# Dealing attention pieces into an expert-layer kernel by need, loading the first weights ahead of other transfers, and a last chunk of 128 tokens laid on partitions

## The chip, the cores and the metric

The kernel runs on one core of one Trainium2 chip. A core has a matrix engine (PE, with its weight loads shown as PEld), a vector engine (DVE), a scalar engine (ACT), a general engine (POOL) and a queue engine (SP) that issues transfers. [...] The metric is device time in microseconds (us), lower is better. A gain or loss counts as one from 0.5% on.

## The reference, cut to what matters

Two blocks run one after the other. The first is a polynomial attention without softmax; its output, with the heads side by side, is the token matrix `x` of 4352 tokens by 128 columns. The second is a sum over four experts, each a two-layer network of inner width 1024, weighted by normalised probabilities of each token.

```python
# q, k, v: (4, 4, 1088, 32); S1, S2: (8, 32)
def phi(x):
    a = np.einsum('rd,bhsd->bhsr', S1, x)
    b = np.einsum('rd,bhsd->bhsr', S2, x)
    return np.einsum('bhsi,bhsj->bhsij', a, b).reshape(*x.shape[:-1], 64)
q_p, k_p = phi(q), phi(k)
kv = np.einsum('bhsf,bhsd->bhfd', k_p, v)
z = np.sum(k_p, axis=2)
num = np.einsum('bhsf,bhfd->bhsd', q_p, kv)
den = np.einsum('bhsf,bhf->bhs', q_p, z)[..., None] + 1e-06
x = (num / den).transpose(0, 2, 1, 3).reshape(4352, 128)
# domain_probs: (4352, 4); w1: (4, 128, 1024); w2: (4, 1024, 128)
p = domain_probs / (domain_probs.sum(-1, keepdims=True) + 1e-09)
out = sum(p[:, e:e+1] * (np.maximum(x @ w1[e], 0) @ w2[e]) for e in range(4))
```

## The kernel before, in words

All data are 32-bit floats. The order of work on each engine is the order in which the Python code emits it (`manual_schedule`); each engine goes through its own list and waits where an operand is not there yet, and everything behind the waiting instruction waits with it. DMA issues stand in the lists of SP and ACT in the same way.

**Expert layer.** The 4352 tokens are columns of `xT` (feature on the partition), cut into chunks: 256, 416, 416, six of 512, and 192. A chunk takes 16 steps, four for each expert; a step handles 256 of the 1024 hidden features. `first(i)` makes the hidden values: for two blocks `j` of 128 features, the product `h` (weights from `w1_sb`), its rectified copy on ACT (L587), and sums and differences of its two token halves on DVE (L571). `second(i)` multiplies them by `w2`: the two token halves and two feature blocks are combined so that seven half-width products stand in for eight. For that `w2s` holds sums of blocks of `w2`, made on POOL by `weight_sums` (L477). The loop emits `second` two steps behind `first` (`LA = 2`). After the four steps of an expert, `gather` copies the two accumulators `o0`, `o1` out on ACT (`ev`), combines them on POOL (`yz`, `ev`, `ct`), multiplies by the gate (the normalised probability, broadcast over partitions by a DMA) and adds to `total`. After the last expert `turn_back` transposes on DVE into `ob` (L651) and SP stores four strips for each batch touched (L655).

The last chunk is "plain": eight full products instead of seven halves, hidden values on DVE alone with the gate multiplied in (L578), all four experts summed in one accumulator, then one transpose and four DMAs, two on SP and two on ACT.

**Attention.** It fills `xT` ahead of the experts. `start()` does the keys of batch 0 and the first 256 tokens, before any expert step. The rest is a Python generator, `front()`, of 260 pieces: 17 for the keys of each later batch and 19 for each unit of 352 to 416 query columns. A piece is one or two instructions (or none, where a gap is left): the transposed queries `qT`, a product with `sq` (tile `f`), three shuffles and an addition on DVE (`qf`, `qb`, `qa`), four products `qp`, the matmuls `den` and `num`, then `dT`, `rc`, `rb` and at last the piece that writes the unit's columns of `xT` (L429). `work()` is called twice a step, after each block `j`, and takes one piece each time (in chunk 0 three pieces in two steps). Before a chunk begins, the loop makes sure of its columns:

```python
while have[0] < START[m] + CHUNKS[m]:
    next(pieces)
```

Those pieces then stand one behind the other in the lists, with no expert work between them. In the profile each f32 matmul has two rows of its own, so a step has 8 rows of `h` and 14 of `o` (8 in the plain chunk); in the order listings below each matmul stands once.

**Transfers at the start.** SP issues the loads of keys, queries and values, then `w1` of expert 0. It then stores the gates (two of four batches; ACT stores the other two), loads the gate of chunk 0, and only then `w2` of expert 0 and the other weights. POOL makes the four `w2s` sums of expert 0 first and then copies the small matrix `sq` (L522), which the second query unit needs.

## Time and profile before

| | |
|---|---|
| time, median of 3 runs | 515.83 us (515.75 to 517.74) |
| the profiled execution: its time, its span | 517.37 us, 515.5 us |
| PE busy | 497.6 us, 97% of the span |
| DVE, ACT, POOL busy | 328.8, 237.2, 232.4 us |
| mean granted PE clock | 0.987 of full speed |

The profile is of one execution. Its span runs from the first to the last instruction; 1.87 us lie around it. Busy shares say little where an engine waits only now and then: what counts is which engine the others wait for at a given place. PE is the engine with almost no idle time, so the reading is a search for the places at which it stands still or runs at a lower clock.

### The profile page before, as it was taken

How to read it: one execution, taken by the hardware profiler on the slowest of the kernel's cores; microseconds unless marked ns; L12 is line 12 of the kernel's file. 1: busy time of each engine (PE TensorE's matmuls, PEld its weight loads, DVE VectorE, ACT ScalarE, POOL GpSimd, SP SyncE). 2: the span in 40 equal slices, each digit the busy share in tenths (PEclk: the TensorE clock that was granted, in tenths of full speed). 3: DMA queues.
4: the chain of work that ended last, by engine and by line, in shares of the span. 5: the costliest groups of instructions: out<-in, count | busy, mean ns of one | idle time of the engine just before them, and what ended most of it. 6: DMA issues, size and time to landing. Idle time of an engine off the chain costs nothing.

```text
span 515.5 us, 10496 instructions
## 1 busy us (share of the span) xinstructions
PE 497.6 (97%) x4178; PEld 356.1 (69%) x4178; DVE 328.8 (64%) x772; ACT 237.2 (46%) x463; POOL 232.4 (45%) x262
## 2 busy tenths in 40 slices
PE   8799999999989999999969999999999999999997
PEld 5477887877745577777625567777777777777786
DVE  7597777586948647476655765557576665454443
ACT  3255456454535454545504455444454455555410
POOL 6565335443534354324442445543555264526560
PEclk9999999999989999999969999999999999999999
DMA  6960123021002202021000210021000300011000
GB/s 186 320 203 2 67 56 88 3 81 18 2 1 81 61 3 86 2 83 21 1 0 1 83 22 0 1 80 25 2 0 6 98 0 2 2 34 18 1 17 14
DMA packets 30176, 22.85 MB, mean 44 GB/s; under 512 B 20784, under 2 KB 27184, under 8 KB 29616
## 3 DMA queue, kind: packets, MB, share of 16 engines
q1 hardware_dynamic: 28912, 21.76, 14.7%
q8 instruction: 33, 0.54, 0.4%
q10 hardware_dynamic: 1216, 0.42, 0.3%
q14 instruction: 15, 0.12, 0.1%
HBM read 19.87 MB, written 2.31 MB: 43 GB/s over the span
## 4 chain that ended last, share of the span: by engine, by line
PE 67%; DVE 2%; POOL 2%; ACT 0%; issue 0%; POOLq 0%; DVEq 0%
PE h L172 35%; PE o L172 27%; PE f L172 3%; POOL ct L686 1%; PE den L172 1%; PE num L172 1%; DVE qp L395 1%; POOL ev L686 1%; DVE hid L571 0%; POOLq L761 0%; POOL total L686 0%; POOL yz L674 0%; ACT hid L587 0%; DVE rb L425 0%; DVE xT L429 0%
## 5 line engine op out<-in xcount | busy, mean ns | idle before, releaser
L571 DVE SCALAR_TENSOR_TENSOR hid<-h,hid 128x256 f32<-128x256 f32 (+4 forms) x432 | 205.4, 476 | 161.0 <-ACT hid L587 153.9
L172 PE MATMUL h<-xT,w_sb 128*64 128x512 f32 (+3 forms) x1280 | 300.3, 535 | 7.3 <-DVE xT L429 5.3
L587 ACT ACTIVATE hid<-h 128x512 f32<-128x512 f32 (+2 forms) x288 | 160.1, 556 | 227.3 <-PE h L172 174.9
L172 PE MATMUL o<-hid,w2s 128*64 128x256 f32 (+2 forms) x1152 | 227.1, 359 | 0.0
L172 PE MATMUL o<-hid,w_sb 128*64 128x256 f32 (+3 forms) x992 | 200.1, 355 | 0.0
L172 PEld LDWEIGHTS h<-xT,w_sb 128*64 128x64 f32 x1280 | 140.4, 138 | 67.7 <-issue 18.0
L172 PEld LDWEIGHTS o<-hid,w2s 128*64 128x64 f32 x1152 | 132.2, 137 | 33.2 <-issue 2.1
L172 PEld LDWEIGHTS o<-hid,w_sb 128*64 128x64 f32 x992 | 111.1, 137 | 29.6 <-issue 9.7
L686 POOL TENSOR_TENSOR ev<-yz,sh 64x256 f32<-64x256 f32 (+2 forms) x72 | 49.5, 687 | 170.4 <-ACT sh L689 167.6
L674 POOL TENSOR_TENSOR yz<-ev 128x512 f32<-128x512 f32 (+2 forms) x36 | 43.2, 1201 | 78.1 <-ACT ev L677 77.7
L686 POOL TENSOR_TENSOR ct<-ev 128x512 f32<-128x512 f32 (+2 forms) x36 | 42.3, 1176 | 2.8
L686 POOL TENSOR_TENSOR ct<-ct,gate 128x512 f32<-128x512 f32 (+2 forms) x27 | 33.1, 1226 | 2.1
L686 POOL TENSOR_TENSOR total<-total,ct 128x512 f32<-128x512 f32 (+2 forms) x27 | 32.7, 1211 | 2.1
L395 DVE TENSOR_TENSOR qp<-qa,qb 64x352 f32<-64x352 f32 (+2 forms) x44 | 31.9, 725 | 1.0
L676 ACT COPY ev<-o 128x512 f32<-128x512 f32 (+2 forms) x36 | 19.6, 545 | 15.3 <-PE o L172 15.1
L677 ACT COPY ev<-o 128x512 f32<-128x512 f32 (+2 forms) x36 | 19.7, 546 | 2.4 <-PE o L172 0.3
L172 PE MATMUL den<-qp,kvz 128*64 128x352 f32 (+3 forms) x48 | 13.9, 501 | 3.9 <-DVE qp L395 3.2
L578 DVE SCALAR_TENSOR_TENSOR hid<-h,gate 128x192 f32<-128x192 f32 x32 | 10.8, 355 | 10.0 <-PE h L172 9.7
L689 ACT COPY sh<-yz 64x256 f32<-64x256 f32 (+2 forms) x36 | 13.8, 382 | 2.3 <-POOL yz L674 1.5
L690 ACT COPY sh<-yz 64x256 f32<-64x256 f32 (+2 forms) x36 | 13.8, 383 | 0.9
L337 DVE TENSOR_TENSOR kp<-fs 128x256 f32<-128x256 f32 (+1 forms) x24 | 14.2, 590 | 0.0
L172 PE MATMUL num<-qp,kvz 128*64 128x352 f32 (+3 forms) x48 | 13.6, 497 | 0.0
(97 smaller groups left out, 218.7 us busy)
## 6 DMA issues: line engine op xcount, KB each, us to landing
w_sb<-in_moe_w_dram SPq DMA_DIRECT2D x8, 512.0 KB, 8.0
gate<-gates SPq DMA_DIRECT2D x4, 1024.0 KB, 4.7
kn<-in_k_dram SPq DMA_DIRECT2D x4, 544.0 KB, 3.9
qn<-in_q_dram SPq DMA_DIRECT2D x4, 544.0 KB, 3.7
vn<-in_v_dram SPq DMA_DIRECT2D x14, 128.0 KB, 4.4
gate<-gates SPq DMA_DIRECT2D x2, 832.0 KB
out_dram<-ob SPq DMA_DIRECT2D x16, 64.0 KB, 1.9
gate<-gates SPq DMA_DIRECT2D x1, 896.0 KB
```

What stands on the lines that cost most here:

```text
L172: nc.tensor.matmul(out(s), weights(s), moving(s), **flags)
L337: eng.tensor_tensor(out=_ap(kps[b], 0, P, 256 * t0 + P * p + 64 * x, [[256, n], [32, 2], [R, 4], [1, R]]), in0=in0, in1=_ap(fss[b], 0, P, ...
L395: nc.vector.tensor_tensor(out=qp[p][64 * x : 64 * x + 64, 0:n], in0=qa[64 * p : 64 * p + 64, 0:n], in1=qb[64 * p : 64 * p + 64, 0:n], op=A ...
L571: nc.vector.scalar_tensor_tensor(out=out, in0=src, scalar=0.0, in1=in1, op0=ALU.max, op1=ALU.subtract)
L578: nc.vector.scalar_tensor_tensor(out=by_blocks(hd, n, n * j), in0=by_blocks(hp, n), scalar=0.0, in1=gate_of(m, e), op0=ALU.max, op1=ALU.mult,)
L587: nc.scalar.activation(hd[:, n * j : n * j + n], hp[:, 0:n], ACTF.Relu)
L674: add = lambda out, in0, in1, op=ALU.add: nc.gpsimd.tensor_tensor(out=out, in0=in0, in1=in1, op=op)
L676: nc.scalar.copy(_ap(ev, 0, P, 0, [[2 * w, 2], [1, w]]), _ap(a0, 0, P, 0, two))
L677: nc.scalar.copy(_ap(ev, 0, P, w, [[2 * w, 2], [1, w]]), _ap(a1, 0, P, 0, two))
L686: add = lambda out, in0, in1, op=ALU.add: nc.gpsimd.tensor_tensor(out=out, in0=in0, in1=in1, op=op)
L689: nc.scalar.copy(sh[HP:P, 0:w], yz[0:HP, 0, 0:w])
L690: nc.scalar.copy(sh[0:HP, 0:w], yz[HP:P, 1, 0:w])
```

## The change

1. The chunks are 256, 416, 416, five of 512, 320, 256 and 128: eleven instead of ten, 176 steps instead of 160. Only the last, of 128 tokens, is plain.
2. Pieces are dealt by a rate. For each chunk a count `needed` says how many pieces must be done for its columns. At each step the rate is set so that every later chunk has its count, and four pieces more, when it begins; `work()` adds half the rate to a credit and takes a piece for each whole unit of credit, at most two. Following the arithmetic, chunks 0 to 9 get 23, 37, 37, 37, 37, 27, 28, 23, 11 and 0 pieces (before: 24, then 32 in each of chunks 1 to 6 and 30 in chunk 7, with 4 forced ahead of chunk 3 and 10 ahead of chunk 5). No piece is forced any more. In chunks 1 to 4 five calls of each chunk take two pieces; before, no call took more than one.
3. `w1` and `w2` of experts 0 and 1 are issued on SP right behind the values. The four stores of the gates and the load of gate 0 go to ACT's list. POOL copies `sq` ahead of the first `w2s` sums.
4. The plain chunk has tokens on partitions: one rectifying instruction a step, on DVE and ACT in turn, for both blocks; the hidden values are the stationary operand and `w2` the moving one. Each expert has its own accumulator, and DVE multiplies it by the token's probability (a number per partition, `p_last`) and adds it to the output tile, which one DMA of 128 rows of 512 bytes stores. `p_last` is loaded and normalised in chunks 8 and 9.
5. The transposition of the chunk ahead of the last one is emitted four steps later.

Core of the diff:

```diff
-    CHUNKS = [256, 416, 416] + [512] * 6 + [192]
+    CHUNKS = [256, 416, 416] + [512] * 5 + [320, 256, P]
...
-    load_w1(0)
+    for e in range(2):
+        load_w1(e)
+        load_w2(e)
...
     def store_gates():
         nc.vector.transpose(pt[:, :], pn[:, :])
         for b in range(B):
-            (nc.sync, nc.scalar)[b % 2].dma_start(
+            nc.scalar.dma_start(
...
-        load_gate(0)
-        load_w2(0)
-        load_w1(1)
-        load_w2(1)
+        load_gate(0, nc.scalar)
         for e in range(2, E):
...
+        for h in range(H):
+            nc.gpsimd.tensor_copy(_ap(sq, ...), _ap(s_T, ...))
         for _ in weight_sums(0):
             pass
-        for h in range(H):
-            nc.gpsimd.tensor_copy(_ap(sq, ...), _ap(s_T, ...))
...
+        if plain(m):                                   # in first()
+            hp = psum(ps_h, "h")
+            for j in range(2):
+                both(hp[:, n * j : n * j + n], w1_sb[:, e, P * (2 * f + j) : P * (2 * f + j + 1)],
+                     xT[:, START[m] : START[m] + n], start=True, stop=True)
+            src = _ap(hp, 0, P, 0, [[n, 2], [32, n // 32], [1, 32]])
+            turned = _ap(hd, 0, P, 0, [[n, 2], [1, n // 32], [n // 32, 32]])
+            if kq % 2:
+                nc.vector.tensor_scalar(out=turned, in0=src, scalar1=0.0, scalar2=None, op0=ALU.max)
+            else:
+                nc.scalar.activation(turned, src, ACTF.Relu)
...
+            for j in range(2):                         # in second(), plain
+                for _ in range(2):
+                    on_side(
+                        lambda s: acc[m][half[s], 0:DM],
+                        lambda s: hd[:, n * j + HP * s : n * j + HP * s + HP],
+                        lambda s: w2_sb[:, e, 2 * f + j, :],
+                        start=(f == j == 0), stop=(f == NP - 1 and j == 1))
+            if f == NP - 1:                            # one DVE instruction per expert
+                ... last = acc[m] * p_last[:, e] (+ last)
...
+    needed, columns, count = [0] * NC, UNITS[0][0], 0
+    for b in range(B):
+        count += 17 if b else 0
+        for n in UNITS[b] if b else UNITS[0][1:]:
+            count, columns = count + 19, columns + n
+            for m in range(NC):
+                if columns - n < START[m] + CHUNKS[m] <= columns:
+                    needed[m] = count
...
+            gone = START[m] + CHUNKS[m] * kq / NQ
+            rate = CHUNKS[m] / NQ * max([0] + [(needed[c] + 4 - done[0]) / (START[c] - gone) for c in range(m + 1, NC)])
             def work():
-                count[0] += 1
-                if m or kq % 2 or count[0] == 2:
-                    next(pieces, None)
+                credit[0] = min(credit[0] + rate / 2, 2)
+                while credit[0] >= 1:
+                    credit[0] -= 1
+                    piece()
...
-    turn_back(NC - 1, acc[NC - 1][:, 0 : CHUNKS[-1]], (nc.sync, nc.scalar))
+    nc.sync.dma_start(bass.AP(out.tensor, ..., [[G * DM, 32], [1, 4 * DM]]), total[NC - 1][:, 0:DM])
```

What this does to the lists of the engines, at three places.

DVE, before, at the border between chunk 4 and chunk 5 (tokens 2112 on): `hid` rows are expert work, the others are pieces of the query unit that ends at column 2912.

```order
L395 TENSOR_TENSOR qp_2664<-qa,qb 64x352
L395 TENSOR_TENSOR qp_2665<-qa,qb 64x352
L454 STREAM_SHUFFLE qa<-qf 128x352
L395 TENSOR_TENSOR qp_2664<-qa,qb 64x352
L395 TENSOR_TENSOR qp_2665<-qa,qb 64x352
L417 STREAM_TRANSPOSE dT<-den 128x352
L420 TENSOR_SCALAR rc<-dT 128x11
L423 RECIPROCAL rc<-rc 128x11
L425 STREAM_TRANSPOSE rb<-rc 128x352
L429 TENSOR_TENSOR xT<-num,rb 128x352
L571 SCALAR_TENSOR_TENSOR hid<-h,hid 128x256
```

DVE, after, at the same unit; this now stands in steps 11 to 13 of chunk 4.

```order
L589 SCALAR_TENSOR_TENSOR hid<-h,hid 128x512
L589 SCALAR_TENSOR_TENSOR hid<-h,hid 128x256 x2
L589 SCALAR_TENSOR_TENSOR hid<-h,hid 128x512
L589 SCALAR_TENSOR_TENSOR hid<-h,hid 128x256 x2
L438 STREAM_TRANSPOSE dT<-den 128x352
L589 SCALAR_TENSOR_TENSOR hid<-h,hid 128x512
L589 SCALAR_TENSOR_TENSOR hid<-h,hid 128x256
L441 TENSOR_SCALAR rc<-dT 128x11
L444 RECIPROCAL rc<-rc 128x11
L446 STREAM_TRANSPOSE rb<-rc 128x352
L589 SCALAR_TENSOR_TENSOR hid<-h,hid 128x256
L450 TENSOR_TENSOR xT<-num,rb 128x352
```

The products, the four rows `dT` to `rb` and the row that writes `xT` stood together; now up to six `hid` rows lie between one group and the next, and `xT` is written more than two steps ahead of the chunk that reads it.

POOL, before, from the last key products of `start()` on.

```order
L337 TENSOR_TENSOR kp<-fs 128x4x64 x2
L337 TENSOR_TENSOR kp<-fs 128x5x64
L477 TENSOR_TENSOR w2s<-w_sb 128x4x64
L477 TENSOR_TENSOR w2s<-w2s,w_sb 128x4x64
L477 TENSOR_TENSOR w2s<-w_sb 128x4x64
L477 TENSOR_TENSOR w2s<-w_sb,w2s 128x4x64
L522 COPY sq<-s_T 32x32 x4
```

POOL, after, the same stretch.

```order
L358 TENSOR_TENSOR kp<-fs 128x4x64 x2
L358 TENSOR_TENSOR kp<-fs 128x5x64
L538 COPY sq<-s_T 32x32 x4
L498 TENSOR_TENSOR w2s<-w_sb 128x4x64
L498 TENSOR_TENSOR w2s<-w2s,w_sb 128x4x64
L498 TENSOR_TENSOR w2s<-w_sb 128x4x64
L498 TENSOR_TENSOR w2s<-w_sb,w2s 128x4x64
```

The four copies that fill `sq` moved from behind the four `w2s` sums of expert 0 to ahead of them.

DVE, before, at the end of the program: the plain chunk of 192 tokens, and the transposition of the 512-token chunk ahead of it (`ob<-total`).

```order
L571 SCALAR_TENSOR_TENSOR hid<-h,hid 128x256
L578 SCALAR_TENSOR_TENSOR hid<-h,gate 128x192 x14
L651 STREAM_TRANSPOSE ob<-total 128x512
L578 SCALAR_TENSOR_TENSOR hid<-h,gate 128x192 x18
L651 STREAM_TRANSPOSE ob<-o_4503 128x192
```

DVE, after, at the end: the plain chunk of 128 tokens, and the transposition of the 256-token chunk.

```order
L589 SCALAR_TENSOR_TENSOR hid<-h,hid 128x128
L605 TENSOR_SCALAR hid<-h 128x2x4x32 x3
L650 TENSOR_SCALAR ob<-o_4879,p_last 128x128
L605 TENSOR_SCALAR hid<-h 128x2x4x32 x2
L655 SCALAR_TENSOR_TENSOR ob<-o_4935,p_last,ob 128x128
L698 STREAM_TRANSPOSE ob<-total 128x256
L605 TENSOR_SCALAR hid<-h 128x2x4x32 x2
L655 SCALAR_TENSOR_TENSOR ob<-o_4981,p_last,ob 128x128
L605 TENSOR_SCALAR hid<-h 128x2x4x32
L655 SCALAR_TENSOR_TENSOR ob<-o_5033,p_last,ob 128x128
```

The row `ob<-total` moved from behind the seventh of 16 steps of the plain chunk to behind the eleventh, and the last row of DVE is a multiply-and-add instead of a transposition.

More of the change, by code (lines that the diff above doesn't have):

```diff
@@ L121 @@
     )
+    p_last = cpool.tile([P, E], F32, name="p_last")
+    p_sum = cpool.tile([P, 3], F32, name="p_sum")
     w1_sb = cpool.tile([P, E, F], F32, name="w1_sb")
@@ L605, in second @@
         if plain(m):
-            if kq == 0:
-                acc[m] = psum(ps_o, "o0")
+            if f == 0:
+                acc[m] = psum(ps_o, f"o{e % 2}")
             for j in range(2):
-                both(
-                    acc[m][:, 0:n],
-                    w2_sb[:, e, 2 * f + j, :],
-                    hd[:, n * j : n * j + n],
-                    start=(kq == j == 0),
-                    stop=(kq == NQ - 1 and j == 1),
-                )
+                for _ in range(2):
[3 more added lines that the diff above has]
+                        lambda s: w2_sb[:, e, 2 * f + j, :],
+                        start=(f == j == 0),
+                        stop=(f == NP - 1 and j == 1),
+                    )
+            if f == NP - 1:
+                if e == 0:
+                    last = mpool.tile([P, CW], F32, tag="ob", name="ob")
+                    total[m] = last
+                    nc.vector.tensor_scalar(
+                        out=last[:, 0:DM], in0=acc[m][:, 0:DM], scalar1=p_last[:, 0:1], scalar2=None, op0=ALU.mult
+                    )
+                else:
+                    last = total[m]
+                    nc.vector.scalar_tensor_tensor(
+                        out=last[:, 0:DM],
+                        in0=acc[m][:, 0:DM],
+                        scalar=p_last[:, e : e + 1],
+                        in1=last[:, 0:DM],
+                        op0=ALU.mult,
+                        op1=ALU.add,
+                    )
             return
@@ L703, in gather_rest, with piece @@
             yield
-            turn_back(m, total.pop(m)[:, 0:n], (nc.sync,))
+            for _ in range(0 if m + 2 < NC else 4):
+                yield
+            turn_back(m, total.pop(m)[:, 0:n])
     start()
     pieces = front()
+    done, credit = [0], [0]
+    def piece():
+        done[0] += 1
+        next(pieces, None)
+    needed, columns, count = [0] * NC, UNITS[0][0], 0
[6 more added lines that the diff above has]
+                    needed[m] = count
     to_sum = chain.from_iterable(weight_sums(e) for e in range(1, E))
```

80 lines of the change are left out of this document (50 added, 30 removed).

## The prediction

> **What bounds the kernel now.** The page comes first: busy shares and the granted clock.
>
> ```profile
> PE 497.6 (97%) x4178; PEld 356.1 (69%) x4178; DVE 328.8 (64%) x772; ACT 237.2 (46%) x463; POOL 232.4 (45%) x262
> PEclk9999999999989999999969999999999999999999
> ```
>
> PE is the bound. The clock row has two dips, an 8 and a 6, in a kernel whose PE is busy all the time otherwise. Busy time by stretches of 10 us finds them:
>
> ```profile
> 140.00:150.00 10.00, 7.49 (x40) 3.56 (x38) 5.88 (x12) 1.56 (x3) 4.58 (x5) 0.83 0.00 0
> 260.00:270.00 10.00, 7.89 (x18) 2.45 (x20) 5.12 (x9) 0.72 (x2) 3.23 (x3) 0.50 0.00 0
> 440.00:450.00 10.00, 10.00 (x74) 7.22 (x71) 4.91 (x10) 5.80 (x11) 3.80 (x5) 1.00 0.01 2
> ```
>
> The second number of a row is PE's busy time, the third from the end its clock. At 260 to 270 PE does 18 matmul rows at half clock; the last row is a calm stretch, with 74. The waits of PE say what for:
>
> ```profile
> PE h L172 <- DVE xT L429: 5.3, 3, 2.5
> PE den L172 <- DVE qp L395: 3.2, 1, 3.2
> PE f L172 <- POOL sq L522: 1.3, 1, 1.3
> PE h L172 <- DVE hid L578: 1.1, 1, 1.1
> PE h L172 <- DVE hid L571: 0.9, 3, 0.4
> ```
>
> The numbers are us in total, times, longest. The first two are attention pieces, forced in a row at a chunk's border (but for one wait for `xT`, that of the kernel's first `h`); the third is the start, the fourth the tail. The fifth is the one to remember: expert work on DVE hardly ever holds PE up.
>
> **The change, part by part.** *The two borders.* The chain of waits around the larger one, then three ordinary rows of it:
>
> ```profile
> 254.31 1.73 PE h L172 x8
> 266.16 3.68 PE h L172 x8
> 271.61 0.64 PE h L172 x2
> ...
> 165.44 1.72 PE h L172 x8
> 168.65 1.81 PE h L172 x8
> 173.08 1.72 PE h L172 x8
> ```
>
> From 254.31 to 271.61 PE starts two steps, with one `den`/`num` group in the first: 17.30 us. Ordinarily a step takes 168.65 - 165.44 = 3.21 and one with such a group 173.08 - 168.65 = 4.43, together 7.64. The border costs 17.30 - 7.64 = 9.66 us. At 266.16 the eight `h` rows take 3.68 instead of 1.72: the half clock outlasts the gap. For the smaller border the timeline and the chain:
>
> ```profile
> 134.68 1.74 PE L172 MATMUL h<-xT,w_sb 128*64 128x416 f32 x8
> 137.31 1.74 PE L172 MATMUL h<-xT,w_sb 128*64 128x416 f32 x8
> 144.31 3.45 PE L172 MATMUL h<-xT,w_sb 128*64 128x512 f32 x8 [2.51 <-DVE xT L429]
> 147.76 1.21 PE o L172 x13
> 148.65 0.59 PE L172 MATMUL h<-xT,w_sb 128*64 128x512 f32 x1
> ```
>
> 137.31 to 148.65 is 11.34. Expected: a 416-step of 137.31 - 134.68 = 2.63, the group's 4.43 - 3.21 = 1.22, a 512 `h` block of 1.72, an `o` block of 1.21, in all 6.78. This border costs 4.56. Dealt by need, no piece is forced, `xT` is written five pieces ahead of its border, and from `qp` to `den` there are two calls of `work()` or more, as at the units that do not stall today. Both costs go: **-14.2 us**.
>
> *What the pieces bring instead.* The work is the same; 148 pieces instead of 142 fall into chunks 1 to 4, with 20 calls that take two. The DVE is fullest in chunk 2:
>
> ```profile
> 95.37:144.31 48.94, 46.43 (x380) 35.74 (x376) 38.02 (x89) 23.93 (x50) 25.49 (x28) 1.00 0.09 27
> ```
>
> It has 36 pieces now, four of them forced, and 37 then. Even if all of its 38.02 us grew with them it were 39.1, of 48.94 - 3.2 = 45.7: it fits, so what is left is lateness inside a step. A double call puts one more DVE piece ahead of the next `hid`. Below, that costs nothing (single calls cost PE 0.9 us in the whole run); a gain is excluded, since nothing waits less. Above, each of 20 doubles costs the longest such wait, 0.4: 8 us. I take 0.03 each, **+0.6**, nearer the lower end, since two steps lie between `hid` and its reader.
>
> *The start.*
>
> ```profile
> 12.20 0.43 SPq L129 DMA_DIRECT2D w_sb<-in_moe_w_dram  x1
> 17.32 1.25 ACT L587 ACTIVATE hid<-h 128x256 f32<-128x256 f32 x3 [6.22 <-PE h L172]
> 18.25 0.73 POOL L477 TENSOR_TENSOR w2s<-w_sb 128x256 f32<-128x256 f32 x1 [6.47 <-DMA w_sb<-in_moe_w_dram]
> 21.10 0.96 POOL L522 COPY sq<-s_T 32x32 f32<-32x32 f32 x4
> 21.61 1.07 PE L172 MATMUL f<-qT,sq 128*64 128x416 f32 x3 [1.29 <-POOL sq L522]
> ```
>
> POOL waits 6.47 us for `w2` of expert 0, and `sq` stands behind its sums. Copied ahead, `sq` is there before 14; `f` then starts when PE is free at 21.61 - 1.29 = 20.32. Late next could be the `w2s` sums, 2.9 us of POOL (18.25 to 21.10): they are done by 20.3 if `w2` lands by 17.4. Issued at 12.20 it was there at 18.25, 6 us on; now it is issued behind the values, before 9. The gain may be given back later in chunk 0, or be larger, since `f` waits a second time within those rows. Bounds 0 and 2.0; I take **-1.3**, the wait itself. ACT now issues four gate stores and the gate load, the last two of them after weight loads that they wait for; ACT's next work is the first `hid` at 17.32. Up to there the issues are covered, and each us beyond is a us on the path, since the `h` buffers wait for that `hid`.
>
> *The tail.*
>
> ```profile
> 498.44 0.33 PE L172 MATMUL h<-xT,w_sb 128*64 128x192 f32 x1
> 499.27 0.71 DVE L651 STREAM_TRANSPOSE ob<-total 128x512 f32<-128x512 f32 x1 [1.96 <-POOL total L686]
> 501.30 0.82 PE L172 MATMUL h<-xT,w_sb 128*64 128x192 f32 x8
> 502.60 0.82 PE L172 MATMUL h<-xT,w_sb 128*64 128x192 f32 x8
> 511.92 0.38 DVE L651 STREAM_TRANSPOSE ob<-o 128x192 f32<-128x192 f32 x1 [1.59 <-PE o L172]
> 512.34 0.87 ACTq L655 DMA_DIRECT2D out_dram<-ob  x2
> L676 ACT COPY ev<-o 128x512 f32<-128x512 f32 (+2 forms) x36 | 19.6, 545 | 15.3 <-PE o L172 15.1
> L571 DVE SCALAR_TENSOR_TENSOR hid<-h,hid 128x128 f32<-128x128 f32 x32 | 8.9, 286 | 6.8 <-ACT hid L587 6.1
> ```
>
> DVE stands in `ob<-total` waiting for POOL, the plain chunk's `hid` behind it, and PE behind that: 501.30 - 498.44 = 2.86 for a step that takes 502.60 - 501.30 = 1.30. With the transposition four steps later and 256 columns on POOL the 1.56 goes. New: the plain chunk's first `o` waits for ACT to empty `o0` with only a short `h` block between; between 0 and 1.1 (two ACT copies of 0.545), I take 0.2, the buffer being needed half a step after its copy can start. Net **-1.4**. The rectified values of a step of the new plain chunk are one row of 256 columns, on ACT (1.25 / 3 = 0.42 at the start) and DVE in turn; two steps of 0.87 (16 rows of 128 columns) hide each. At the very end 0.38 of transposition becomes a DVE row of 0.29, and of two DMA issues (0.87) one goes: **-0.5**, bounds 0 and -0.6.
>
> *Matmul time.* Columns per step over all chunks stay, but for 64 tokens that move from eight products to seven: per token and step 8 rows of `o` become 14 half rows. At 1.30 / 16 rows of 192 columns, 0.42 ns a column, that is 64 x 16 x 0.42 = 0.43 us less. One more chunk adds 16 steps of 22 rows, each with a weight load. Whether short matmuls cost more than their columns is seen in chunk 0 and in `start()`:
>
> ```profile
> 11.08 2.30 PE L172 MATMUL f<-vx,kp 128*64 128x66 f32 x72
> 41.69 0.27 PE L172 MATMUL o<-hid,w_sb 128*64 128x128 f32 x1
> 42.56 0.38 PE L172 MATMUL h<-xT,w_sb 128*64 128x256 f32 x2
> ```
>
> 72 rows of 66 columns, each with its load, take 32 ns each, a few ns above their columns. The 14 `o` rows of 128 columns and one `h` row start within 42.56 - 41.69 = 0.87 us, and at 0.42 ns a column they come to 0.86. A few ns times 352 new rows is at most 1: **0** in sum, bounds -0.4 and +1. [...]
>
> *The rest.* `p_last` is one SP issue, three POOL and two DVE rows of at most 128 x 4 elements in chunks 8 and 9, where DVE has 11 pieces and none: hidden by the steps there. SP's weight loads of experts 0 and 1 move ahead of the gates; what SP issues behind them (the other weights, batch 1) keeps its order and moves forward. Nothing for either.
>
> *Sum:* -14.2 + 0.6 - 1.3 - 1.4 - 0.5 = **-16.8**. The profiled execution took 517.37, so 500.6. It lies 1.54 above the median of 515.83; of the runs some are near 515.8 and one at 517.74, and a shift by one longer spell of half clock would look so. I put all of it down to the borders, so it vanishes in the new kernel: **500.6 us**.
>
> **The rivals.** *Doubles crowd the DVE (a new wait in place of the old).* For it: DVE at 83% of chunk 2. Against: the 0.9 us above. Price: the upper bound, +8 instead of +0.6, so 508. *Short matmuls are bound by their loads.* A load row lasts 137 ns:
>
> ```profile
> L172 PEld LDWEIGHTS o<-hid,w2s 128*64 128x64 f32 x1152 | 132.2, 137 | 33.2 <-issue 2.1
> ```
>
> Over two column halves that is 69 ns, against 54 for 128 columns. Price for 480 rows: 7.2 us, so 507.8. Against: the 32 ns above. [...] *A border stalls still,* because DVE falls behind its list: one of 4.56, 505. *The weights come no sooner, or ACT's issues hold up its first `hid`:* 502 to 504. *Slower:* the lateness does not vanish but moves to `den` in the four units of chunks 1 to 4 whose pieces are doubled; where PE waits there as long as at the smaller border (2.51 us), the clock falls again. Four times 4.56 is 18.2, and 500.6 + 18.2 = 518.8. [...]
>
> **How the numbers follow.** Forecast 0.70 (its own range 498.5 to 503); crowding 0.12; a border still 0.06; start or ACT 0.06; load-bound matmuls 0.04; slower 0.02. 497 to 507 leaves out most of the crowding, half of the load-bound case and the slower one, some 2 in 10 at most; its lower end is the start's and the pieces' bounds together with a border of 1.5 us more. 0.5% is 2.6 us: faster 0.95, same 0.02, slower 0.03.
>
> **What the profile after would show.** Right: a clock row without dips, mean near 1.0; no wait of PE for `xT`, `qp` or `sq`; DVE's `ob<-total` without a wait that PE sees; PE's `h` blocks 3.2 us apart (4.4 with `den`) through the borders at tokens 1088 and 2112; a span near 499. Wrong: PE waits for `hid` (L589) of more than 3 us in sum, in chunks 1 to 4; `o` rows of 128 columns above 60 ns apart; ACT's first `hid` later than 17.3; a dip of the clock anywhere.

## The result, and the profile after

The changed kernel takes 500.12 us, the median of four runs (500.05 to 500.77). Beside it the kernel before took 515.79 (four runs, 514.29 to 517.74), a ratio of 0.9697 with a 95% interval of 0.9663 to 0.973. The forecast was 500.6. The profiled execution took 500.12 us, with a span of 498.2.

The mean granted clock of an execution of the kernel before lies between 0.980 and 0.997 in all sessions, and its time between 514.3 and 522.7 us with it (one execution of 1064.4 us is left out), while the four runs of the kernel after lie within 0.72 us.

The page after, busy shares and the clock row:

```profile
PE 489.8 (98%) x4530; PEld 369.4 (74%) x4530; DVE 333.6 (67%) x802; ACT 252.6 (51%) x519; POOL 239.3 (48%) x288
PEclk9999999999999999999999999999999999999999
```

PE has 352 rows more and is busy for 7.8 us less: rows at half clock had counted as busy time. The two dips of the clock are gone; its record stands at a half only from 496.97 on, after the last matmul. The same stretches of 10 us as before, and chunk 2 (busy time of PE, PEld, DVE, ACT, POOL, then the clock):

```profile
140.00:150.00 10.00, 10.00 (x78) 7.09 (x76) 6.97 (x19) 4.86 (x9) 5.50 (x6) 1.00 0.01 2
260.00:270.00 10.00, 10.00 (x70) 7.18 (x68) 7.49 (x18) 4.79 (x9) 5.22 (x5) 1.00 0.01 2
94.72:140.42 45.70, 45.70 (x378) 36.03 (x376) 35.43 (x89) 23.94 (x50) 22.42 (x24) 1.00 0.09 29
```

PE never stops in them. Chunk 2 takes 45.70 instead of 48.94. All waits of PE (us in total, times, longest):

```profile
PE h L177 <- DVE xT L450: 1.8, 1, 1.8
PE h L167 <- DVE warm L139: 1.2, 1, 1.2
PE h L177 <- DVE hid L589: 0.7, 2, 0.4
PE den L177 <- DVE kvz L379: 0.6, 1, 0.6
PE f L177 <- ACT fs L347: 0.5, 1, 0.5
```

The wait for `xT` is now one, that of the kernel's first `h`. `qp`, `sq` and the plain chunk's `hid` are gone from the list. The last row is new: it is a product of batch 1's keys in chunk 1. The chain of waits through the border at token 2112, where chunk 5 begins at 252.90:

```profile
249.46 1.72 PE h L177 x8
251.18 0.59 PE f L177 x4
251.77 1.33 PE o L177 x13
253.11 1.89 PE h L177 x8
255.00 1.51 PE o L177 x13
256.51 1.72 PE h L177 x8
258.23 1.33 PE o L177 x13
259.56 1.89 PE h L177 x8
```

PE goes from step to step, 3.1 to 3.7 us apart, with the product `f` of a later unit between, and waits for nothing. The start, in five rows of four engines:

```profile
11.69 0.97 POOL L538 COPY sq<-s_T 32x32 f32<-32x32 f32 x4
14.92 0.72 POOL L498 TENSOR_TENSOR w2s<-w_sb,w2s 128x256 f32<-128x256 f32 x1
15.24 0.42 DVE L441 TENSOR_SCALAR rc<-dT 128x8 f32<-128x8 f32 x1
17.66 0.82 ACT L615 ACTIVATE hid<-h 128x256 f32<-128x256 f32 x2 [6.67 <-PE h L177]
20.49 0.87 PE L177 MATMUL f<-qT,sq 128*64 128x416 f32 x4
```

`sq` is there at 12.66 and `f` starts without a wait. The first `hid` is at 17.66, since the first `h` starts at 16.96 instead of 16.62. The tail, rows of DVE:

```profile
488.69 0.32 DVE L655 SCALAR_TENSOR_TENSOR ob<-o,p_last,ob 128x128 f32<-128x128 f32 x1
488.94 0.43 DVE L698 STREAM_TRANSPOSE ob<-total 128x256 f32<-128x256 f32 x1
494.86 0.35 DVE L655 SCALAR_TENSOR_TENSOR ob<-o,p_last,ob 128x128 f32<-128x128 f32 x1 [0.76 <-PE o L177]
```

The transposition follows the row ahead of it at once; only the kernel's very last row waits, for PE.

Where the 17.2 us between the two spans went is worked out from the starts of the `h` rows: what a chunk takes, from its first `h` to that of the next, less the columns of the matmul rows in it at 3.20 us for 7,680 of them (0.4167 ns each). That rate is an estimate from calm steps of 512, which have 7,680 columns: one took 3.21 us before, two neighbours after (`h` from 301.53, 304.72 and 307.98 on) 3.19 and 3.26. It is the same on both sides. The rows of the key products, 64 or 66 columns each, are taken at 32 ns, as 72 of them took in `start()`.

| us | before | after | difference |
|---|---|---|---|
| the first `h` starts | 16.62 | 16.96 | +0.34 |
| lost in chunk 0 | 5.05 | 2.77 | -2.28 |
| lost in chunk 1 | 0.24 | 0.90 | +0.66 |
| lost in chunks 2 and 3 (border at token 1088) | 5.46 | 0.62 | -4.84 |
| lost in chunks 4 and 5 (border at token 2112) | 10.47 | 0.77 | -9.70 |
| lost in chunks 6 to 8 | 1.27 | 1.23 | -0.04 |
| lost in the rest (one chunk before, two after) | 1.73 | 0.99 | -0.74 |
| all columns | 470.70 | 470.30 | -0.40 |
| start of the last matmul to the end | 3.92 | 3.71 | -0.21 |
| span | 515.46 | 498.25 | -17.2 |

### The profile page after: what moved, and what is told of

Same layout as the page of the kernel before. It is cut to its first block, busy times and chain, and to the rows that moved or that the text cites. A ratio compares the mean times of both kernels' runs of the same rounds, so it can differ in the third digit from the quotient of the medians.

```text
span 498.2 us, 11354 instructions
## 1 busy us (share of the span) xinstructions
PE 489.8 (98%) x4530; PEld 369.4 (74%) x4530; DVE 333.6 (67%) x802; ACT 252.6 (51%) x519; POOL 239.3 (48%) x288
## 3 DMA queue, kind: packets, MB, share of 16 engines
q1 hardware_dynamic: 28608, 20.98, 14.6%
## 4 chain that ended last, share of the span: by engine, by line
PE 97%; DVE 1%; ACT 0%; issue 0%; DVEq 0%
PE h L177 48%; PE o L177 40%; PE f L177 5%; PE den L177 2%; PE num L177 2%; PE h L167 1%; DVE hid L589 1%; DVE qp L416 0%; ACT hid L615 0%; DVE kvz L379 0%; DVE dT L438 0%; DVE rb L446 0%; DVE xT L450 0%; DVE rc L441 0%; ACT fs L347 0%
## 5 line engine op out<-in xcount | busy, mean ns | idle before, releaser
L589 DVE SCALAR_TENSOR_TENSOR hid<-h,hid 128x256 f32<-128x256 f32 (+6 forms) x480 | 214.6, 448 | 144.6 <-ACT hid L615 134.4
L177 PE MATMUL h<-xT,w_sb 128*64 128x512 f32 (+4 forms) x1408 | 299.2, 496 | 2.7 <-DVE xT L450 1.8
L615 ACT ACTIVATE hid<-h 128x512 f32<-128x512 f32 (+3 forms) x320 | 167.2, 523 | 211.7 <-PE h L177 166.9
L177 PE MATMUL o<-hid,w2s 128*64 128x256 f32 (+3 forms) x1280 | 232.0, 342 | 0.0
L731 POOL TENSOR_TENSOR ev<-yz,sh 64x256 f32<-64x256 f32 (+3 forms) x80 | 51.7, 646 | 164.5 <-ACT sh L734 161.5
L719 POOL TENSOR_TENSOR yz<-ev 128x512 f32<-128x512 f32 (+3 forms) x40 | 44.3, 1108 | 67.0 <-ACT ev L722 66.8
L731 POOL TENSOR_TENSOR ct<-ev 128x512 f32<-128x512 f32 (+3 forms) x40 | 44.1, 1102 | 3.1
L731 POOL TENSOR_TENSOR ct<-ct,gate 128x512 f32<-128x512 f32 (+3 forms) x30 | 33.6, 1119 | 2.3
L731 POOL TENSOR_TENSOR total<-total,ct 128x512 f32<-128x512 f32 (+3 forms) x30 | 33.2, 1108 | 2.4
L721 ACT COPY ev<-o 128x512 f32<-128x512 f32 (+3 forms) x40 | 20.4, 511 | 9.1 <-PE o L177 8.4
L722 ACT COPY ev<-o 128x512 f32<-128x512 f32 (+3 forms) x40 | 20.5, 512 | 2.4
L734 ACT COPY sh<-yz 64x256 f32<-64x256 f32 (+3 forms) x40 | 14.6, 366 | 1.5 <-POOL yz L719 0.5
L735 ACT COPY sh<-yz 64x256 f32<-64x256 f32 (+3 forms) x40 | 14.6, 366 | 1.0
L177 PE MATMUL den<-qp,kvz 128*64 128x352 f32 (+3 forms) x48 | 11.4, 470 | 0.6 <-DVE kvz L379 0.6
```

Source lines behind the costliest of these rows:

```text
L177: nc.tensor.matmul(out(s), weights(s), moving(s), **flags)
L589: nc.vector.scalar_tensor_tensor(out=out, in0=src, scalar=0.0, in1=in1, op0=ALU.max, op1=ALU.subtract)
L615: nc.scalar.activation(hd[:, n * j : n * j + n], hp[:, 0:n], ACTF.Relu)
L719: add = lambda out, in0, in1, op=ALU.add: nc.gpsimd.tensor_tensor(out=out, in0=in0, in1=in1, op=op)
L721: nc.scalar.copy(_ap(ev, 0, P, 0, [[2 * w, 2], [1, w]]), _ap(a0, 0, P, 0, two))
L722: nc.scalar.copy(_ap(ev, 0, P, w, [[2 * w, 2], [1, w]]), _ap(a1, 0, P, 0, two))
```

## The experiments

The kernels stand in three groups. The first takes the change apart, the second takes single causes apart, and the third tests the prices that the forecast had only bounded. A ratio is that to the kernel before on the same chip; the kernel before had medians of 516.1, 516.6 and 516.5 us there. The kernel after was not run beside them, so a difference from its 500.12 us is one between sessions.

### The parts alone

**rate_only**: the kernel before with the new dealing (the counting of `needed` and the line of `rate` are as in the diff above).

```diff
...
-                count[0] += 1
-                if m or kq % 2 or count[0] == 2:
-                    next(pieces, None)
+                credit[0] = min(credit[0] + rate / 2, 2)
+                while credit[0] >= 1:
+                    credit[0] -= 1
+                    piece()
```

> The kernel before with the dealing by need alone (old chunks, old start, old tail). Theory: the two borders are worth 14.5 us and the double calls cost 0.7, so 515.8 - 13.8 = 502.0 (501.0 to 503.0), a clock row without dips, the waits for sq (1.3) and for hid in the plain chunk (1.1) still there. Rival: the shorter last chunks are what frees the DVE, and the dealing alone leaves a gap somewhere: 505 or more, with a dip of the clock.

Measured: 504.76 (503.45 to 507.23), ratio 0.9781 (0.9755 to 0.9806). In the profiled run the clock row is flat at 9, and of PE's waits these are left:

```profile
PE h L172 <- DVE xT L429: 1.6, 1, 1.6
PE f L172 <- POOL sq L522: 1.1, 1, 1.1
PE h L172 <- DVE hid L578: 1.1, 1, 1.1
```

Both borders are gone by the dealing alone: chunks 2 to 5 lose 1.21 us in this trace, against 15.93 before. So the rival that the short chunks free DVE is out. But the time is above the expected range. The likely reason is that it had taken the half clock behind the borders for a part of every execution; the median execution of the kernel before has less of it than the profiled one, and the clock falls in some runs of rate_only too: its six have mean clocks of 0.993 to 1.0, and the two at 1.0 took 503.45 and 504.22 us.

**start_only**: the kernel before with the loads, the gate issues and `sq` moved.

```diff
-    load_w1(0)
+    for e in range(2):
+        load_w1(e)
+        load_w2(e)
...
-        load_gate(0)
-        load_w2(0)
-        load_w1(1)
-        load_w2(1)
+        load_gate(0, nc.scalar)
...
-        for _ in weight_sums(0):
-            pass
         for h in range(H):
             nc.gpsimd.tensor_copy(_ap(sq, ...), _ap(s_T, ...))
+        for _ in weight_sums(0):
+            pass
```

> The kernel before with the whole change of the start alone (weights of experts 0 and 1 ahead, gate stores and gate 0 on ACT, sq copied ahead of the w2s sums). Theory: start gains 1.5 (1.9 at the first steps, 0.3 given back because the first h begins later), so 514.3 (513.8 to 514.8). Rival: the gap at the first border swallows it, since what the border waits for is DVE's chain and not PE: 515.8, no change.

Measured: 514.12 (511.81 to 516.41), ratio 0.9952 (0.9931 to 0.9973), 2.0 us less. The gain is not swallowed at the border: in its trace chunk 0 loses 3.08 instead of 5.05, though its first `h` starts at 17.54 instead of 16.62.

**tail_only**: the kernel before with the new chunks, the new plain chunk and the later transposition.

```diff
-    CHUNKS = [256, 416, 416] + [512] * 6 + [192]
+    CHUNKS = [256, 416, 416] + [512] * 5 + [320, 256, P]
...
+            for _ in range(0 if m + 2 < NC else 4):
+                yield
-            turn_back(m, total.pop(m)[:, 0:n], (nc.sync,))
+            turn_back(m, total.pop(m)[:, 0:n])
```

> The kernel before with the new chunks, the new plain chunk and the later transposition, but the old dealing (forced pieces) and the old start. Theory: the wait of 1.35 at the tail and about 0.3 at the end go, so 515.8 - 1.7 = 514.1 (513.5 to 514.7); both borders and their clock dips stay. Rival: the shorter chunks cost 1 us or more in weight loads, so 515 to 516.

Measured: 514.91 (513.35 to 517.6), ratio 0.9971 (0.9952 to 0.999), 1.2 us less. The expected value lies inside the interval, and so does a part of the rival's range, so the time does not decide between them; the trace has no wait for `hid` in the plain chunk any more.

**no_rate**: the kernel after with the old dealing.

```diff
-                credit[0] = min(credit[0] + rate / 2, 2)
-                while credit[0] >= 1:
-                    credit[0] -= 1
-                    piece()
+                count[0] += 1
+                if m or kq % 2 or count[0] == 2:
+                    next(pieces, None)
```

> The kernel after with the old dealing: one piece a call and forced pieces at the borders. Theory: 500.1 + 13.8 = 513.9 at most; the sum of start and tail alone is worth 1.5 + 1.7, so 512.6 (512.0 to 514.0). Both borders' gaps and dips are back. Rival: the loads issued sooner and the free queue shorten the borders too: 508 to 511.

Measured: 514.43 (510.41 to 515.86), ratio 0.9951 (0.9924 to 0.9978). That is 0.4 above the expected range. Three of the eleven executions took 510.41 to 511.29, inside or next to the rival's range; they are those with a mean clock of 0.997, and the kernel after with the two gaps alone (3.1 and 7.2 us, worked out below) would take 510.4. So it is the clock that differs in them, and nothing shows that the borders got shorter. In the profiled run waits and clock are back as before the change:

```profile
PE h L177 <- DVE xT L450: 5.3, 3, 2.5
PE den L177 <- DVE qp L416: 3.2, 1, 3.2
PEclk9999999999989999999969999999999999999999
```

The dealing is worth 514.43 - 500.12 = 14.3 us on top of the rest, and 516.14 - 504.76 = 11.4 alone. The three parts alone add up to 11.4 + 2.0 + 1.2 = 14.6; together they gave 15.7. The times with a border in them carry a spread of 4 to 5 us, so this difference of 1.1 is not much; it has the sign that a clock falling at any gap that is left would give, which is not shown.

### Single causes

**sq_first** and **weights_early** split the start: the first is the kernel before with `sq` ahead of the sums and nothing else, the second moves the loads and the gate issues and leaves `sq` behind the sums.

```diff
# sq_first
-        for _ in weight_sums(0):
-            pass
         for h in range(H):
             nc.gpsimd.tensor_copy(_ap(sq, ...), _ap(s_T, ...))
+        for _ in weight_sums(0):
+            pass
```

> The kernel before; only POOL's four copies of sq stand ahead of the w2s sums. Theory: the order on POOL alone makes the wait for sq (1.3 to 1.5 us), since POOL waited 6.5 us for w2 anyway; it goes, the w2s sums still end near 21.2, just ahead of the first o: 1.3 to 1.9 less, 516.1 to 514.5 (513.8 to 515.0), and the first h is not later. Rival: the late w2s sums take the wait's place (o waits for w2s by 1 us or more): 515.5 or more.

```diff
# weights_early
-    load_w1(0)
+    for e in range(2):
+        load_w1(e)
+        load_w2(e)
...
-        load_gate(0)
-        load_w2(0)
-        load_w1(1)
-        load_w2(1)
+        load_gate(0, nc.scalar)
```

> The kernel before; only the loads and the gate issues are moved, sq stays behind the w2s sums. Theory: the sums now run from about 13 to 17 and sq follows before 18, ahead of its reader at 20.3: the same 1.3 to 1.9 less, but the sums lie beside DVE's rows of the first tokens, so the rc row takes 0.4 or more instead of 0.17 and the first h comes 0.3 later: 514.7 (514.0 to 515.3). Rival: the loads land no sooner, because the transfers of the start share the bandwidth: PE still waits for sq, 516.

Measured: sq_first 516.88 (513.52 to 517.83), ratio 1.0001 (0.998 to 1.0023); weights_early 514.21 (512.3 to 516.17), ratio 0.9954 (0.9933 to 0.9976). The wait for `sq` is gone from both traces, and none for `w2s` has come. weights_early did as expected; the median of sq_first is no lower. Its profiled run shows what else there was, by stretches of 1 us:

```profile
16.00:17.00 1.00, 0.00 (x0) 0.00 (x0) 0.82 (x4) 0.00 (x0) 0.00 (x0) 1.00 0.96 280
17.00:18.00 1.00, 0.53 (x4) 0.35 (x6) 0.42 (x1) 0.00 (x0) 0.00 (x0) 0.80 1.05 350
18.00:19.00 1.00, 1.00 (x8) 0.61 (x6) 0.02 (x1) 0.38 (x1) 0.00 (x0) 0.50 0.97 362
20.00:21.00 1.00, 1.00 (x8) 0.55 (x6) 0.97 (x3) 0.38 (x1) 1.00 (x2) 0.50 1.17 332
21.00:22.00 1.00, 1.00 (x12) 0.57 (x10) 0.47 (x3) 0.77 (x2) 1.00 (x2) 0.99 1.05 377
```

The clock stands at a half from 17.6 to 21.0, behind PE's wait for the first `xT`. In the 3.41 us ahead of this fall PE was busy for 1.21; in the kernel before, whose first `h` came at 16.62 and not at 17.47, it was busy for 1.84 from 14.28 to 17.69, and the clock held. Even so chunk 0 loses 3.90 instead of 5.05 in this trace; the later first `h` takes most of that back. Its twelve runs have mean clocks of 0.983 (four), 0.987 (three), 0.99 (two) and 0.993 (three), lower than the kernel before beside it (19 of 34 at 0.993 or more). At equal mean clock sq_first is the faster one: at 0.993 its three runs took 513.52 to 515.09 us and 14 of the kernel before 514.59 to 516.79, at 0.99 its two took 515.53 and 516.23 and six 516.90 to 517.67.

**warm_border** and **warm_sq_first** test this. The first is the kernel before with two bf16 products on unused data behind each forced piece but the last of a border; the second has `sq` ahead of the sums too.

```diff
             while have[0] < START[m] + CHUNKS[m]:
                 next(pieces)
+                if have[0] < START[m] + CHUNKS[m]:
+                    wp = psum(ps_h, "h")
+                    for _ in range(2):
+                        nc.tensor.matmul(wp[:, :], warm[:, 0:P], warm[:, :], start=True, stop=True)
```

> The kernel before with two short bf16 products on unused data behind each forced piece but the last (3 and 9 times 2, about 0.4 us a pair), so that PE is not idle all through the borders. Theory: the border costs two things, the gap itself (3.2 and 7.8 us, in every execution) and half clock after it (1.5 to 2.1 us, in some executions only). If the products hold the clock, only the second goes: 514.4 and little spread, waits for xT and qp unchanged; if they are too few, 516 as before. Rival: the whole border is lost clock, so 505 to 508.

> warm_border with sq copied ahead of the w2s sums. sq_first alone did not move the median, though its wait is gone; its runs had a lower mean clock. If that is so (a half clock window of 3.4 us, 1.7 us lost, met more often), then with the clock held at the borders the gain shows: 514.2 - 1.5 = 512.7 (512.0 to 513.4). If the w2s sums, which are as late as before, simply take the wait's place, 514.2 as in warm_border.

Measured: warm_border 514.23 (513.64 to 516.73), ratio 0.9975 (0.9957 to 0.9992), so 1.3 us less by the ratio and 2.4 by the medians; warm_sq_first 512.41 (512.25 to 513.06), ratio 0.99 (0.9852 to 0.9948). The stretches of warm_border at the larger border, the last two those in which the kernel before had gone on at 0.50:

```profile
261.00:262.00 1.00, 0.74 (x2) 0.13 (x2) 1.00 (x1) 0.00 (x0) 1.00 (x1) 1.00 0.00 0
266.00:267.00 1.00, 1.00 (x7) 0.38 (x5) 0.00 (x0) 0.17 (x1) 0.00 (x0) 1.00 0.00 0
267.00:268.00 1.00, 1.00 (x10) 0.66 (x8) 0.54 (x2) 0.79 (x2) 0.00 (x0) 1.00 0.00 0
```

The clock is held through both borders, and what goes is the half clock only: the step ahead of the border at token 2112 still takes 11.55 us (12.19 before), the one ahead of token 1088 6.86 (7.00), while the `h` blocks behind them run at full speed. So a border is two things. The gap is DVE's chain of forced pieces, 3.1 and 7.2 us (up to 0.6 more where the clock falls inside it), and it is there in each trace that has forced pieces. The half clock costs 1.5 and 2.1 us behind them in the kernel before (half of 144.31 to 147.40 and of 266.16 to 270.28), and it is there in some executions: in start_only's trace, with a mean clock of 0.997, the first steps of chunks 3 and 5 lose next to nothing, in no_rate's, at 0.985, 1.69 and 2.10. The spread of warm_border is not as little as expected: nine of its twelve runs have a mean clock below 1.0, and in the profiled one the clock falls at 22.1, behind the wait for `sq`. With the borders held, `sq` ahead of the sums is worth 514.23 - 512.41 = 1.8 us, though these two are from different chips; runs at a mean clock of 1.0 alone say the same, 514.06 to 514.25 (three) against 512.25 to 512.51 (five). The order on POOL alone therefore removes the wait and its price; that sq_first showed no gain goes with the lower clock of its runs, and why they met more half clock than the kernel beside it, or why the first `h` of the profiled one was late, stays open.

**ob_later**: the kernel before with the transposition alone four steps later.

```diff
             yield
+            for _ in range(0 if m + 2 < NC else 4):
+                yield
             turn_back(m, total.pop(m)[:, 0:n], (nc.sync,))
```

> The kernel before; only the transposition of the chunk ahead of the last one is emitted four steps later. Theory: the wait of DVE for total (1.96) and PE's 1.5 behind it go: 516.1 to 514.6 (514.0 to 515.1). Rival: the transposition's stores end later and their landing becomes the end of the kernel: 516 or more.

Measured: 515.96 (513.52 to 517.29), ratio 0.9979 (0.9957 to 1.0001): inconclusive by time. By the trace the plain chunk loses 0.42 instead of 1.73, so 1.3 us of the tail is this edit's, and the end (3.92 us from the last matmul's start) is as before, so the stores behind it do not set it.

### The prices

**bunch**: the kernel after, pieces only in pairs.

```diff
-                credit[0] = min(credit[0] + rate / 2, 2)
-                while credit[0] >= 1:
-                    credit[0] -= 1
-                    piece()
+                credit[0] = min(credit[0] + rate / 2, 4)
+                if credit[0] >= 2 - 1e-9:
+                    credit[0] -= 2
+                    piece()
+                    piece()
```

> The kernel after, but a call of work() takes no piece until it can take two: all 260 dealt pieces now come in pairs, about 110 more double calls. Theory: two steps lie between a hid row and its reader, so a double call costs 0.03 at most: 500.5 to 503.5, waits for hid below 3 us in all. Rival: each double call holds up the next hid by 0.4 us that PE feels: 500.1 + 110 x 0.4 = 544, and clock dips.

Measured: 507.7 (507.42 to 508.44), ratio 0.981 (0.9758 to 0.9863), that is 7.6 us more than the kernel after for some 110 more double calls, 0.07 each. Neither side was right: the price is twice the theory's and a sixth of the rival's, and it is not even. By the trace (7.3 more in the span, with the first `h` 0.3 sooner) 1.3 fall in chunk 0, 1.9 in chunk 1, 2.1 in chunk 2, 1.0 in chunk 3, 1.5 in chunks 5 and 8, and 0.1 at most in each of chunks 4, 6, 7, 9 and 10. What PE waits for, above 0.7 and behind the kernel's first `h`:

```profile
PE f L177 <- ACT fs L347: 1.4, 3, 0.5
PE h L177 <- DVE hid L589: 1.3, 2, 1.0
PE f L177 <- DVE kp L358: 0.9, 1, 0.9
PE den L177 <- DVE qp L416: 0.8, 1, 0.8
```

Three of the four are not the next `hid` but the pieces' own chain: a piece for PE that is taken close behind the piece it needs. In chunk 2, where DVE is fullest, it comes to a standstill of another kind. Rows of the chain that ended last there:

```profile
127.75 0.42 DVE qp L416
128.19 1.31 DVE qp L416
129.53 0.39 DVE hid L589
...
133.58 1.18 DVE qp L416
134.80 0.51 PE den L177
```

The chain runs on DVE for 10 us, and two of four equal `qp` rows take 1.2 to 1.3 us instead of 0.5, while POOL adds up an expert's result (more on this at the end).

**split512**: the kernel after with one more chunk border.

```diff
-    CHUNKS = [256, 416, 416] + [512] * 5 + [320, 256, P]
+    CHUNKS = [256, 416, 416] + [512] * 4 + [256, 256] + [320, 256, P]
```

> The kernel after with one chunk of 512 tokens cut into two of 256: the same columns in 16 steps more, with 448 o rows of 128 columns in place of 224 of 256, 256 h rows of 256 in place of 128 of 512. Theory: a row costs its columns and a few ns, and a chunk of 256 loses 0.48 to an ideal of columns alone as one of 512 does: 500.1 + 0.5 to 0.9 = 500.6 to 501.0. [...]

Measured: 500.87 (500.49 to 502.51), ratio 0.9679 (0.9632 to 0.9727), 0.75 us more than the kernel after for 352 rows more, or 2 ns a row (from the first `h` on, the two traces differ by 0.9). The page of it:

```profile
PE 490.6 (98%) x4882; PEld 387.9 (78%) x4882; DVE 340.1 (68%) x851; ACT 260.3 (52%) x567; POOL 242.8 (49%) x311
```

PEld gains 18.5 us of busy time and PE 0.8. Loads do not bind rows of 128 columns here.

**tidy**: the kernel after with two small edits, looked for in their own rows.

```diff
-        for _ in weight_sums(0):
-            pass
...
         for _ in attend(b, 0, n, qp):
             pass
+        nc.gpsimd.tensor_copy(p_sum[:, 0:1], xT[:, 0:1])
+        for _ in weight_sums(0):
+            pass
...
-                nc.vector.tensor_scalar(out=turned, in0=src, ...)
+                nc.vector.tensor_scalar(out=hd[:, 0 : 2 * n], in0=hp[:, 0 : 2 * n], ...)
...
-                nc.scalar.activation(turned, src, ACTF.Relu)
+                nc.scalar.activation(hd[:, 0 : 2 * n], hp[:, 0 : 2 * n], ACTF.Relu)
...
-        bass.AP(out.tensor, ..., [[G * DM, 32], [1, 4 * DM]]),
+        bass.AP(out.tensor, ..., [[DM, 4], [G * DM, 32], [1, DM]]),
```

> The kernel after with two edits that touch different rows. First, POOL's w2s sums of expert 0 wait (behind a copy of one column of xT) until the first tokens are written; second, the rectified rows of the last chunk are written contiguously, and the strides stand in the two transfers of p_last and of the output instead. Theory: rc falls from 0.42 to 0.17 and the first h starts 0.25 to 0.35 earlier, the sums still end before their reader at 21.2; the rectified rows fall from 0.65 to about 0.39 but were hidden: 499.8 (499.5 to 500.1). Rival: the late sums hold up the first o, or the output's transfer gets slower with the strides: 500.4 or more.

Measured: 500.69 (500.14 to 502.82), ratio 0.9676 (0.9628 to 0.9725): no better than the kernel after. The rectified rows as groups, first of the kernel after, then of tidy (busy, mean ns of one, then the idle time):

```profile
L607 ACT ACTIVATE hid<-h 128x256 f32<-128x256 f32 x8 | 5.2, 647 | 5.9 <-PE h L177 5.5 <-ACT sh L735 0.3
L605 DVE TENSOR_SCALAR hid<-h 128x256 f32<-128x256 f32 x8 | 5.1, 635 | 8.6 <-PE h L177 8.6
```

```profile
L606 ACT ACTIVATE hid<-h 128x256 f32<-128x256 f32 x8 | 3.1, 383 | 7.2 <-PE h L177 6.8 <-ACT sh L734 0.3
L604 DVE TENSOR_SCALAR hid<-h 128x256 f32<-128x256 f32 x8 | 3.4, 425 | 9.5 <-PE h L177 9.5
```

The strided write was what made them long, and shortening them is worth nothing, as the waits had said. `rc` is back at 0.17. The time lies in the rival's range, and the rival has a point: from the end of DVE's last row to the end of the span there are 3.5 us in this trace, and 3.0 in each of four traces with the old pattern (after, no_rate, bunch, split512). That this is the stride of the last transfer is likely but was not tried by itself. In the profiled run the first `h` came only at 18.19: PE had waited 1.2 us for the first keys, whose products start 0.9 us later than in the kernel after, and the clock then stood at a half from 18.3 to 21.7; what the later sums are worth can't be read from it.

## Why the prediction was right

The time and the sign came out, and so did the mechanism and size of the one large term, the borders. That the sum is right to 0.5 us is in part luck: borders (-0.34), start (-0.64) and columns (-0.40) gave more than forecast, tail and end together 0.95 less. By its own steps, against the table above:

- **Two borders, -14.2**: measured -4.84 and -9.70, together -14.5, in the two profiled executions. The mechanism is shown: rate_only removes both, no_rate brings both back. What the step missed is that its price has two parts of different kinds. The gaps are in each execution, the half clock behind them in some, and the profiled execution was one with both. "I put all of it down to the borders" holds within that execution; as a rule for the median it was too much: rate_only took 504.76 where 502.0 was expected.
- **Crowding, +0.6**: measured +0.66, and all of it in chunk 1. The price of 0.03 for each of 20 double calls was right as a sum and wrong as a picture. bunch gives 0.07 a call, none of it in three chunks that take pieces, and most of it not through the next `hid` but through the pieces' own chain. In the kernel after most of it is one place: two pieces of batch 1's keys, taken in one call, after which PE waits 0.5 for `fs` from ACT.
- **Start, -1.3**: measured -2.28 in chunk 0 and +0.34 ahead of it, -1.9 in sum, at the far bound of "0 and 2.0". 1.85 of the 2.28 fall in the step that holds `f` (2.05 lost before, 0.20 after): the wait itself and, as the step had left open, `f` that "waits a second time within those rows". Most of the rest is in later steps of chunk 0 and comes with the dealing: start_only loses 3.08 there, the kernel after 2.77. The +0.34 was in no term. 0.25 of it is `rc`, held up by POOL's sums, which the earlier weights had moved beside it. It is no fixed price: in bunch and split512, with the same start, the first `h` is at 16.63 and 16.67, and over all traces here it lies between 16.62 and 18.19. The sign "ACT's first `hid` later than 17.3" fired at 17.66, but for this reason and not for ACT's issues, the last of which stands at 15.59 for 0.35 us: as a sign for that rival it was badly chosen.
- **Tail, -1.4**: the row "lost in the rest" has -0.74, of which one more chunk's ordinary loss is +0.5; the stall itself is -1.2 to -1.3 (ob_later: 1.73 to 0.42). The wait of 0.2 for `o0` did not come: PE waits for no `ev`.
- **End, -0.5**: -0.21. The last DVE row took 0.35 instead of the 0.29 that was forecast.
- **Matmul time, 0**: columns -0.40, the new chunk's loss +0.5 (it stands in the tail's row above). split512 repeats it with 0.75 us for a chunk more. The rival was priced for 480 short rows in the last two chunks, 224 and 128 of `o` and 128 of `h`, and no run shows a price for load-bound rows: those of the plain chunk stand 54 ns apart (0.87 us for a step of 16), where the rival had 69, and split512 has no sign of a load-bound row.
- **Rectified row, 0.42**: it took 0.64, the one duration that was clearly mis-sized. It came from a contiguous row and the new one writes with a step of four elements; tidy shows 0.38 (ACT) and 0.43 (DVE) without the step. Two steps of 0.87 hid it all the same.

Of the rivals, the borders' stall, the late weights and load-bound matmuls are ruled out by the trace after. Crowding is real and was met at a twelfth of its upper bound; bunch reaches 507.7, near the rival's 508, but only with six times as many double calls.

## What to carry to other kernels

Work that may run at any time before a date, put in ahead of the date in one piece, costs its dependent chain (here 3.1 and 7.2 us); dealt at a rate that meets each date, it costs next to nothing (here 0.7 us for 148 pieces), as long as no call takes two pieces of which the second needs the first. A stall of the matrix engine is priced in two parts, the gap and the clock behind it (here 3.1 and 7.2 us, and 1.5 and 2.1 in some executions): read the gap from the waits, and the clock from several executions, since one profile may show all of it or none. Before an edit of a few tenths of a per cent is judged by time, take away the gaps that let the clock fall, or hold the clock through them; or compare executions of equal mean clock; otherwise the spread hides it, as it hid `sq` ahead of the sums.

## What the runs showed of the hardware

**The clock fell for pieces of 3.4 us, and PE had not been idle all through ahead of them.** It stood at a half from 143.99 to 147.40 and, three such pieces long, from 260.04 to 270.28 in the kernel before, from 17.6 to 21.0 in sq_first, and from 22.1 to 25.5 in warm_border behind its wait for `sq`:

```profile
21.00:22.00 1.00, 0.09 (x1) 0.09 (x2) 0.86 (x4) 0.00 (x1) 0.88 (x4) 1.00 1.07 330
22.00:23.00 1.00, 1.00 (x3) 0.44 (x5) 0.18 (x1) 0.00 (x0) 0.88 (x3) 0.54 1.20 322
24.00:25.00 1.00, 1.00 (x14) 1.00 (x12) 0.00 (x0) 0.00 (x0) 1.00 (x2) 0.50 1.10 341
```

The mean clocks of executions fit such pieces: they stand near 0.997, 0.993, 0.990 and 0.987, steps of 0.0033, and 0.0033 x 515 = 1.7 us is a half of 3.4. In the kernel before the changes of clock lie a whole number of pieces apart: 260.04 to 270.28 is three times 3.413 us, and 147.40 to 260.04 is 33 times that. Counted in such pieces from the start of the span, the falls stand differently from trace to trace: 143.99 in the kernel before is 42 pieces and 0.6 us, 17.6 in sq_first 5 and 0.5, 22.1 in warm_border 6 and 1.6. That this is why the same gap costs clock in some executions and not in others would fit, but is not shown. In the 3.41 us ahead of a fall PE had been busy for 1.2 (first border of the kernel before, sq_first), for 0.95 (its second border) and for up to 1.74 (warm_border); 1.84, from 14.28 to 17.69 in the kernel before, brought no fall. Where the line between them lies, the traces do not show.

**Some rows of DVE that started beside a POOL row ended just behind it.** `rc`, 128 x 8 elements, takes 0.17 us alone (kernel before). Beside a `w2s` sum it took 0.42, 0.66, 0.40 and 0.27 us (after, start_only, weights_early, bunch), and each time it ended 0.02 to 0.04 us behind a sum's row. In start_only the sum and `rc` read:

```profile
15.49 0.72 POOL L479 TENSOR_TENSOR w2s<-w_sb 128x256 f32<-128x256 f32 x1
15.58 0.66 DVE L422 TENSOR_SCALAR rc<-dT 128x8 f32<-128x8 f32 x1
```

The sum ends at 16.21 and `rc` at 16.24. The long `qp` rows of bunch are the same: POOL's rows end at 129.11 and 134.36, and `qp` ends 0.4 us later; a `qp` row of this size (64 x 352) that starts with no POOL row running takes 0.51 or 0.52 in the kernels before and after. The border of the kernel before had them too: at token 2112 three of its `qp` rows took 0.86 to 1.48 us, and each ended 0.4 us behind a row of POOL. What holds these rows is not shown.

**A step of 16 bytes between written elements cost ACT 0.26 us and DVE 0.21 us on rows of 128 x 256** (647 against 383 ns, 635 against 425), with the reading side nearly the same.
